# Three parts instead of two for the last output chunk of an attention and MLP kernel

## The chip, the cores and the metric

The kernel runs on one core of a Trainium2 chip. A core has TensorE (matrix products into PSUM, the accumulator memory), VectorE, ScalarE and GpSimd for element work, and SyncE (SP), whose queue issues the DMA transfers here. The profile calls them PE, DVE, ACT, POOL and SP. Each engine works through its own stream of instructions in order; between engines, semaphores tell what is done. The metric is the device time of one execution in microseconds (us), the median over runs.

## The reference

Eight batches with twelve heads of 448 tokens and 64 dimensions: queries and keys are normalised, attention is computed, the heads are put side by side to 768 columns, and an MLP with the activation h - tanh(h) follows. All is float32.

```python
attn = softmax(scale * rmsnorm(q, g_q) @ rmsnorm(k, g_k).T) @ v      # (8, 12, 448, 64)
x = attn.transpose(0, 2, 1, 3).reshape(3584, 768)
h = x @ w_in                                                         # (3584, 2048)
out = (h - tanh(h)) @ w_out                                          # (3584, 768)
```

## The kernel before

The attention of a head pair of one batch is a step; the MLP of the batches before it is cut up into single matrix products and laid between the attention's work, so that TensorE is nearly always busy. The MLP is computed with hidden units or output columns on the partitions and tokens along the rows, so the output comes out turned: 128 output columns by 448 tokens for each of the six chunks (`CD`) of a batch. It has to be turned back before it is stored.

Batches 2 to 7 are taken in pairs, and their second MLP product is a fast matrix multiplication in two levels: seven outer products `p`, in the order `OUTER = (1, 2, 3, 7, 6, 5, 4)`, each of which has two output chunks by seven inner products `q` (`ORDER`) and a third chunk (`HC - 1`) by one plain product over eight row blocks (`HF`). `project_pair` does this. `matmuls` (L1140) issues the products of one bank, `add` (L1148) is an addition on VectorE, `combine_outer` (L1151) gathers the outer products into `acc` and `acc2` and leaves later work in the lists `calm` and `todo`, which `flush` (L1202) works off, an entry at a time.

The end of the program is the last outer product of the last pair (`p == 4` with `late["ending"]`, L1253). By then four chunks remain. Two of `p == 5` and two of `p == 4` have been turned by VectorE in blocks of 32 by 32 (L1167, L1168, L1172), and ScalarE copies them into rows of 128 columns (`move_rows`, L991 to L999, four copies each), so that a store has runs of 512 bytes. The two stores of `p == 4` wait in `late["rows"]`.

The last chunk, the third one of `p == 4`, goes another way. It is cut by tokens into parts. For each part, the loop of L1259 takes a bank, issues eight products (`matmuls`, L1142), adds the bank to `acc` (L1264, L1149), turns the part straight into rows by four transposes of VectorE, one for each block of 32 columns, and issues its store on SP (`turn_rows`, L1001 to L1008; `store_rows`, L985). The first entry of `late["rows"]` is stored ahead of the loop (L1258), the second one after the first part (L1266). So SP's queue at the end is: the two copied chunks of `p == 5`, the first copied chunk of `p == 4`, the first part, the second copied chunk of `p == 4`, the remaining part.

The three banks of the products are taken in turn (`mm_bank`, L215). Each entry below runs in program order; nothing reorders it (`tc.manual_schedule()`). DMA transfers take eight semaphores in turn, and SP waits for the last use of one before it takes it again. After the program's last store, every engine branches over the code of a second, more general path to the closing code (L1843, L1875).

Of the kernel before, what the change touches and what calls it, by code (L numbers as in the profile page):

```python
# [147 lines left out]
def bounded_path(tc, ctx, q, k, v, moe_w_in, moe_w_out, out, g_col, ident, ones, half_ones, neg_half, early):  # L148
# [18 lines left out]
    B, H, S, D = q.shape  # L167
    DFF, DM = moe_w_out.shape
    P = 128
# [45 lines left out]
    def mm_bank():  # L215
        return bank_of("mm")
# [203 lines left out]
    def ring_load(to):  # L420

        for n in range(len(ring_tiles), min(to, len(ring_steps))):
            b, layer, j, p = ring_steps[n]
            t = ring_tiles[ring_steps[n]] = ring_slot()
            if layer == 0:
                assert kept[1] > j
                nc.sync.dma_start(out=t[:, : 2 * HALF], in_=w_in_dram[j, p])
            elif layer == 2 and p == 0:
                nc.sync.dma_start(out=t, in_=w_out_dram[:, BLOCKS[j], HC - 1].rearrange("p f d -> p (f d)"))
            elif layer == 2:  # L430
                n = min(2 * HB, 7 * HB - 2 * (p - 1) * HB)
                at = 2 * (p - 1) * HB
                nc.sync.dma_start(out=t[:, :n], in_=inner_dram[j][:, at : at + n])
            else:
                nc.sync.dma_start(out=t, in_=w_out_dram[:, BLOCKS[p], j].rearrange("p f d -> p (f d)"))
# [383 lines left out]
    def part(name):  # L819
        if name == "th" and "blocks" in late:  # L820
            late["turn"] = (late.get("turn", 0) + 1) % 3
            if late["turn"] == 0:
                return late["blocks"].tile([P, 2, HS], F32, name="th_more")
        return tp.tile([P, 2, HS], F32, name=name)
# [153 lines left out]
    def row_room():  # L978
        if late["places"] % 4 == 0:
            late["place"] = pp.tile([P, 2, 2, S], F32, name="p", bufs=2)  # L980
        g = late["places"] % 4
        late["places"] += 1
        return late["place"][g * BL : (g + 1) * BL].rearrange("t a b s -> t (a b s)").rearrange("t (j d) -> t j d", d=P)
# [17 lines left out]
    def turn_rows(b, n, y, room, cols):  # L1001

        for i in range(P // BL):
            nc.vector.transpose(
                out=room[:, cols.start // BL : cols.stop // BL, i * BL : (i + 1) * BL],
                in_=y[i * BL : (i + 1) * BL, cols].rearrange("d (j t) -> d j t", t=BL),
            )
        store_rows(b, n, room, cols)  # L1008

    def step_out(by=1):  # L1010
        for entry in late["out"]:
            entry[0] -= by
        while late["out"] and late["out"][0][0] <= 0:
            late["out"].pop(0)[1]()
# [60 lines left out]
    def rows(p, f, n, cols):  # L1075
        which, half = HOME[p]
        return late["pair_g"][which][:, half * HF + f : half * HF + f + n, cols]
# [35 lines left out]
    def project_pair(b, ks):  # L1113
# [15 lines left out]
        def at(k, q):  # L1129

            p = OUTER[k]
            if q in outer_plan.get(p, {}):
                outer_sum(*outer_plan[p][q])
            if k == SOON and q == 1:
                inner_sum(p, 2)
                inner_sum(p, 3)
            if q in inner_at and k + 1 in ks:
                inner_sum(OUTER[k + 1], inner_at[q])

        def matmuls(bank, n, w, moving, first):  # L1140
            for i, mv in enumerate(moving):
                nc.tensor.matmul(  # L1142
                    bank[:, :n], lhsT=w(i), rhs=mv, start=(first and i == 0), stop=(i == len(moving) - 1),
                    skip_group_check=not first,
                )
                yield 4 * n / ENGINE_NS

        def add(out, x, y, op=ALU.add):  # L1148
            nc.vector.tensor_tensor(out=out, in0=x, in1=y, op=op)  # L1149
# [52 lines left out]
        def flush():  # L1202
            now, late["todo"] = late["todo"], []
            for fn in now:
                fn()
            calm_step(p == 4 and q in (3, 7, 4))

        for k in ks:
            p = OUTER[k]
            late["ending"] = b + 2 == B and k >= len(OUTER) - 2  # L1210
            step = ring_steps.index((b, 2, p, 1))
            if p in (1, 3):
                y1, y2 = ((acc if p == 1 else acc2)[:, m] for m in range(2))
            else:
                y1, y2 = (part(n).rearrange("p f s -> p (f s)") for n in ("s2", "s5"))
            s1 = part("s1").rearrange("p f s -> p (f s)")
            banks = {}
            for i, q in enumerate(ORDER):
                ring_load(step + 5 + i // 2)
                step_out()  # L1220
                w = ring_tiles[b, 2, p, 1 + i // 2][:, i % 2 * HB : (i % 2 + 1) * HB].rearrange("p (f d) -> p f d", d=P)
                first = q not in (2, 3, 7)
                bank = banks[q] = mm_bank() if first else banks[{2: 1, 3: 5, 7: 6}[q]]
                if q in (1, 2, 3):
                    moving = [rows(p, KB * (q > 1) + c, 1, high if q == 3 else low)[:, 0] for c in range(KB)]
                else:
                    u = us.pop((p, inner_plan[q])) if q != 5 and q != 6 else us[p, inner_plan[q]]
                    moving = [u[:, c] for c in range(KB)]
                yield from matmuls(bank, HS, lambda c: w[:, c], moving, first)
                flush()  # L1230
                v = bank[:, :HS]
                if q == 1:
                    nc.scalar.copy(out=s1[:, low], in_=v)
                elif q == 5:
                    add(y2[:, low], v, s1[:, low])
                elif q == 6:
                    add(y1[:, high], v, s1[:, low])
                elif q == 2:
                    nc.scalar.copy(out=y1[:, low], in_=v)
                elif q == 7:  # L1240
                    add(y2[:, high], v, y2[:, low])
                    add(s1[:, low], v, s1[:, low])
                elif q == 3:
                    add(y1[:, high], v, y1[:, high])
                    late["todo"].append(lambda p=p, y=y1: combine_outer(p, 0, y))
                elif q == 4:
                    add(y2[:, low], v, s1[:, low])
                    late["todo"].append(lambda p=p, y=y2: combine_outer(p, 1, y))
                at(k, q)
            ring_load(step + 9)  # L1250
            step_out()
            w = ring_tiles[b, 2, p, 0].rearrange("p (f d) -> p f d", d=P)
            if p == 4 and late["ending"]:  # L1253
                while calm or late["todo"]:
                    flush()
                step_out(9)
                y, room = acc[:, HC - 1], row_room()
                late["rows"].pop(0)()  # L1258
                for cols in (slice(0, S - P), slice(S - P, S)):  # L1259
                    bank = mm_bank()  # L1260
                    moving = [rows(p, f, 1, cols)[:, 0] for f in range(HF)]
                    n = cols.stop - cols.start
                    yield from matmuls(bank, n, lambda i: w[:, i], moving, True)
                    add(y[:, cols], bank[:, :n], y[:, cols])  # L1264
                    turn_rows(b, CD - 1, y, room, cols)
                    if late["rows"]:  # L1266
                        late["rows"].pop(0)()
                continue
            bank = mm_bank()
            yield from matmuls(bank, S, lambda i: w[:, i], [rows(p, f, 1, slice(0, S))[:, 0] for f in range(HF)], True)  # L1270
            flush()
            late["todo"].append(lambda p=p, v=bank[:, :S]: combine_outer(p, HC - 1, v))
# [607 lines left out]
```

## Time and profile before

| | |
|---|---|
| median of 3 runs | 1345.73 us (1344.27 to 1347.03) |
| the profiled execution | 1345.78 us |
| its span, first to last instruction | 1344.0 us |
| granted TensorE clock, mean | 0.996 |
| last matmul starts | 1334.17 us |
| VectorE's last instruction ends | 1336.95 us |
| DMA over the span | 187 GB/s |

All times inside the execution are counted from the first instruction. The span is what the profile covers; 1.8 us of the measured time lie around it. A busy share is an average over the whole span, while the change touches its last 16 us alone, so the stages that matter are read from the timeline and from the chain of waits (which follows the end back to what released it). "Idle before" is the time an engine stood still before an instruction, with the instruction it waited for. A DMA issue is listed with the time that SP spent on it; the data move later. The fields of a matrix product are its moving operand's columns: an f32 product of 128 rows comes as two instructions.

### The profile page before, as it was taken

How to read it: one execution, taken by the hardware profiler on the slowest of the kernel's cores; microseconds unless marked ns; L12 is line 12 of the kernel's file. 1: busy time of each engine (PE TensorE's matmuls, PEld its weight loads, DVE VectorE, ACT ScalarE, POOL GpSimd, SP SyncE). 2: the span in 40 equal slices, each digit the busy share in tenths (PEclk: the TensorE clock that was granted, in tenths of full speed). 3: DMA queues.
4: the chain of work that ended last, by engine and by line, in shares of the span. 5: the costliest groups of instructions: out<-in, count | busy, mean ns of one | idle time of the engine just before them, and what ended most of it. 6: DMA issues, size and time to landing. Idle time of an engine off the chain costs nothing.

```text
span 1344.0 us, 29262 instructions
## 1 busy us (share of the span) xinstructions
PE 1311.7 (98%) x11352; PEld 1032.5 (77%) x11352; DVE 965.0 (72%) x1405; ACT 567.8 (42%) x1328; POOL 791.5 (59%) x591
## 2 busy tenths in 40 slices
PE   7988999999999999999999999999999999999997
PEld 3467854488898888688877788779887888799985
DVE  4999978867766677678888576768887667633454
ACT  7855654244333454446322345454512254311102
POOL 4766766348756256826698245944699254812761
PEclk9999999999999999999999999999999999999999
DMA  7879888889989766476655867476645775365544
GB/s 174 193 196 261 267 260 229 246 273 283 326 280 285 190 165 172 118 184 158 175 146 135 202 162 177 124 169 168 179 138 140 150 201 164 111 165 178 171 143 88
DMA packets 364744, 253.54 MB, mean 189 GB/s; under 512 B 273012, under 2 KB 303284, under 8 KB 364596
## 3 DMA queue, kind: packets, MB, share of 16 engines
q1 hardware_dynamic: 364592, 251.57, 67.6%
q8 instruction: 92, 1.51, 0.5%
q14 instruction: 56, 0.46, 0.1%
q10 hardware_dynamic: 4, 0.00, 0.0%
HBM read 205.23 MB, written 46.27 MB: 187 GB/s over the span
## 4 chain that ended last, share of the span: by engine, by line
PE 85%; DVE 5%; POOL 4%; DMA 2%; issue 1%; SPq 1%; ACT 1%; DVEq 0%; ACTq 0%; POOLq 0%
PE mm L857 39%; PE mm L1142 20%; PE sc L569 9%; PE sc L635 6%; PE mm L1339 5%; POOL u L1099 2%; PE sc L623 1%; POOL rr_mine L523 1%; PE mm L677 1%; PE sc L677 1%; PE mm L700 1%; DVE rows L613 1%; DMA qk_nat<-in_q_dram 1%; DMA w_f<-w_in 0%; DVE rows L606 0%
## 5 line engine op out<-in xcount | busy, mean ns | idle before, releaser
L857 PE MATMUL mm<-xT,w_f 128*128 128x224 f32 x1296 | 263.7, 353 | 1.1 <-DMA w_f<-w_in 1.0
L857 PEld LDWEIGHTS mm<-xT,w_f 128*128 128x128 f32 x1296 | 244.7, 190 | 6.1 <-issue 4.0
L569 PE MATMUL sc<-qT,kT 64*32 64x448 f32 (+1 forms) x3072 | 214.7, 500 | 2.8 <-ACT p_last L575 2.2
L857 PE MATMUL mm<-tt,w_f 128*128 128x224 f32 x1044 | 212.7, 355 | 0.0
L857 PEld LDWEIGHTS mm<-tt,w_f 128*128 128x128 f32 x1044 | 195.8, 190 | 15.6 <-issue 15.4
L523 POOL TENSOR_TENSOR rr_mine<-rr_mine,neg_half 128x28 f32<-128x28 f32 x33 | 161.4, 4890 | 2.8
L762 DVE TENSOR_TENSOR xT<-xT,sc 128x448 f32<-128x448 f32 x34 | 21.0, 618 | 165.9 <-PE sc L569 116.6
L1142 PE MATMUL mm<-u,w_f 128*128 128x224 f32 x672 | 137.2, 354 | 1.0 <-POOL u L1099 0.5
L905 POOL TENSOR_TENSOR gT<-s,th 128x448 f32<-128x448 f32 x44 | 57.5, 1308 | 131.8 <-ACT th L904 128.4
L1142 PE MATMUL mm<-gT,w_f 128*128 128x224 f32 (+3 forms) x496 | 132.0, 420 | 1.3 <-DVE acc L1149 0.9
L1142 PEld LDWEIGHTS mm<-u,w_f 128*128 128x128 f32 x672 | 126.1, 190 | 8.0 <-POOL u L1099 3.6
L569 PEld LDWEIGHTS sc<-qT,kT 64*32 64x32 f32 x3072 | 72.1, 106 | 67.3 <-issue 49.6
L1142 PEld LDWEIGHTS mm<-gT,w_f 128*128 128x128 f32 x496 | 92.5, 190 | 35.9 <-issue 32.0
L635 PE MATMUL sc<-p,v_nat 64*32 64x448 f32 x1184 | 116.9, 536 | 0.0
L1142 PE MATMUL mm<-g,w_f 128*128 128x224 f32 (+1 forms) x360 | 98.9, 428 | 0.0
L575 ACT ACTIVATE p<-sc 128x448 f32<-128x448 f32 x132 | 71.7, 543 | 50.4 <-PE sc L569 36.0
L905 POOL TENSOR_TENSOR g<-s,th 128x448 f32<-128x448 f32 x24 | 30.3, 1262 | 104.1 <-ACT th L904 104.1
L1142 PEld LDWEIGHTS mm<-g,w_f 128*128 128x128 f32 x360 | 67.9, 190 | 26.5 <-issue 26.0
L729 ACT COPY sum_g<-sum 32x14 f32<-32x14 f32 x280 | 56.3, 201 | 71.0 <-DVE sum L721 65.3
L1339 PE MATMUL mm<-gT,w_out 128*128 128x448 f32 x192 | 74.0, 542 | 0.0
L145 POOL TENSOR_TENSOR rr<-rr,neg_half 112x8 f32<-112x8 f32 (+1 forms) x30 | 49.4, 1677 | 35.7 <-DVE rr L144 35.2
L1099 POOL TENSOR_TENSOR u<-gT 128x448 f32<-128x448 f32 x48 | 63.4, 1341 | 11.1 <-PE mm L1142 11.1
(206 smaller groups left out, 2461.8 us busy)
## 6 DMA issues: line engine op xcount, KB each, us to landing
w_f<-w_in SPq DMA_DIRECT2D x196, 384.0 KB, 3.4
w_f<-w_inner SPq DMA_DIRECT2D x63, 512.0 KB, 3.6
w_f<-w_out SPq DMA_DIRECT2D x42, 512.0 KB, 4.0
w_raw<-in_moe_w_out_dram SPq DMA_DIRECT2D x16, 768.0 KB, 5.4
w_in<-w_out SPq DMA_DIRECT2D x21, 384.0 KB, 5.2
qk_nat<-in_q_dram SPq DMA_DIRECT2D x132, 56.0 KB, 2.7
qk_nat<-in_k_dram SPq DMA_DIRECT2D x132, 56.0 KB, 2.3
g<-w_out SPq DMA_DIRECT2D x14, 512.0 KB, 5.4
```

Source lines behind the costliest of these rows:

```text
L145: nc.gpsimd.tensor_tensor(out=r, in0=r, in1=neg_half[:rows], op=ALU.pow)
L523: nc.gpsimd.tensor_tensor(out=mine, in0=mine, in1=neg_half[:, :1].to_broadcast([P, 2 * NJ]), op=ALU.pow)
L569: nc.tensor.matmul(tiles[h][i * BL : (i + 1) * BL, :n], lhsT=kT[r, c * P + at : c * P + at + BL], rhs=qT[r, first : first + n], start=True ...
L575: nc.scalar.activation(p[:, h, c if c < 2 else 0, :], tiles[h][:, :n], AF.Exp, scale=1.0 if rr is None else rr[:, 0, 2 * c + h : 2 * c + h ...
L635: nc.tensor.matmul(av[g][i * BL : (i + 1) * BL, :S], lhsT=v_nat[keys, h, c, m * BL : (m + 1) * BL], rhs=p[keys, h], start=first, stop=True ...
L677: nc.tensor.matmul(av[n][r : r + BL, :HS], lhsT=v_nat[:, h, c, m * BL : (m + 1) * BL], rhs=p[c][:, h, n * HS : (n + 1) * HS], start=False, ...
L729: nc.scalar.copy(out=acc[h * BL : (h + 1) * BL, g], in_=part[g * BL : (g + 1) * BL, h * NJ : (h + 1) * NJ])
L857: nc.tensor.matmul(bank[:, f * HS : (f + 1) * HS], lhsT=w[:, c * width + f, :], rhs=moving[p](c), start=(first and f == 0 and c == 0), sto ...
L905: eng.tensor_tensor(out=g[:, rows, cols], in0=h, in1=th, op=ALU.subtract)
L1099: nc.gpsimd.tensor_tensor(out=u[:, half], in0=a[:, half], in1=z[:, half], op=ALU.subtract)
L1142: nc.tensor.matmul(bank[:, :n], lhsT=w(i), rhs=mv, start=(first and i == 0), stop=(i == len(moving) - 1), skip_group_check=not first,)
L1339: nc.tensor.matmul(bank[:, :S], lhsT=w_out_row(f, n // HC)[:, n % HC * P : (n % HC + 1) * P], rhs=g[:, f, :], start=(f == 0), stop=(f == C ...
```

## The change

The loop over the parts of the last chunk runs over three slices of tokens, 192, 128 and 128, where it ran over two, 320 and 128. With `S = 448` and `P = 128`:

```diff
@@ -1256,7 +1256,7 @@
                 step_out(9)
                 y, room = acc[:, HC - 1], row_room()
                 late["rows"].pop(0)()
-                for cols in (slice(0, S - P), slice(S - P, S)):
+                for cols in (slice(0, S - 2 * P), slice(S - 2 * P, S - P), slice(S - P, S)):
                     bank = mm_bank()
                     moving = [rows(p, f, 1, cols)[:, 0] for f in range(HF)]
                     n = cols.stop - cols.start
```

The body of the loop is the same. Each part has its own bank, eight products, an addition, four transposes and a store; the second copied chunk of `p == 4` is still stored after the first part, and so ahead of the second one and the third.

## The prediction

> **What bounds the kernel now.** I read the page first, then the chain of waits of the last 44 us, then the timeline of the last 19 us by shape, and last SP's issues one by one. The page says TensorE, and the chain of waits (start, length, what) says where that stops:
>
> ```profile
> PE 1311.7 (98%) x11352; PEld 1032.5 (77%) x11352; DVE 965.0 (72%) x1405; ACT 567.8 (42%) x1328; POOL 791.5 (59%) x591
> ```
>
> ```profile
> by line: PE mm L1142 75.1%; DVE p L1004 6.8%; DVE acc L1149 1.8%; issue 1.1%
> ...
> 1299.65 33.02 PE mm L1142 x148
> ...
> 1332.70 0.50 DVE acc L1149
> ...
> 1333.23 0.50 DVE p L1004
> ...
> 1335.34 0.30 DVE acc L1149
> ...
> 1336.65 0.30 DVE p L1004
> ```
>
> TensorE carries the chain up to 1332.68. From there it is VectorE: add of 320 columns, four transposes, add of 128, four transposes, to 1336.95. The change lies wholly in this tail, so nothing before 1328.19 can move. The timeline by shape (start, busy, engine, line, what, count):
>
> ```profile
> 1328.19 6.25 PE L1142 MATMUL mm<-gT,w_f 128*128 128x320 f32 x32
> 1328.70 7.01 ACT L995 COPY p<-s 32x448 f32<-32x448 f32 x12
> ...
> 1330.54 0.65 DVE L1172 STREAM_TRANSPOSE s<-acc 128x448 f32<-128x448 f32 x1
> 1332.70 0.49 DVE L1149 TENSOR_TENSOR acc<-mm,acc 128x320 f32<-128x320 f32 x1 [1.52 <-PE mm L1142]
> 1333.23 2.08 DVE L1004 STREAM_TRANSPOSE p<-acc 32x320 f32<-32x320 f32 x4
> 1335.34 0.29 DVE L1149 TENSOR_TENSOR acc<-mm,acc 128x128 f32<-128x128 f32 x1
> 1335.66 1.29 DVE L1004 STREAM_TRANSPOSE p<-acc 32x128 f32<-32x128 f32 x4
> ```
>
> The first row holds both parts (16 instructions of each shape). VectorE idles 1.52 us before the first add: this is what a smaller first part can use. ACT is busy until 1335.71 with the copies of two other chunks, whose stores share SP's queue with ours. SP's single issues:
>
> ```profile
> 1333.39 0.32 SPq L986 DMA_DIRECT2D out_dram<-p  x1
> ...
> 1335.33 0.32 SPq L986 DMA_DIRECT2D out_dram<-p  x1
> ...
> 1335.74 0.41 SPq L986 DMA_DIRECT2D out_dram<-p  x1
> ...
> 1336.98 0.90 SPq L986 DMA_DIRECT2D out_dram<-p  x1
> ...
> 1319.92 1.38 SPq L971 DMA_DIRECT2D out_dram<-s  x1
> ```
>
> In order: the store of the copied chunk 3 (R1), of our 320 tokens, of the copied chunk 4 (R2), of our last 128 tokens, and an older store for comparison. An undisturbed issue takes 0.32 us. The last one took 0.90 us: SP was held 0.58 us. After it SP has only its branch (1337.93) and the closing waits; the first of these ran at 1340.49, the second at 1342.69, and the span ends at 1344.0. So the end follows SP's last issue by 6.1 us (1344.0 - 1337.88), and that issue is the number to predict.
>
> The hold has a visible cause. The DMA view of 1336 to 1337.5 lists instruction packets among the stores:
>
> ```profile
> q8 instruction: 1, 0.02, 4.7%
> q14 instruction: 2, 0.02, 2.6%
> ```
>
> The q8 packet (16 KB, one DMA engine) ran from 1336.36 to 1337.49. On 15 engines our 320-token store had landed by 1337.84, on the sixteenth at 1338.75, and SP's last issue went through at 1337.88, 0.39 us after the packet. The older store shows the same: q8 packet from 1319.57 to 1320.87, the third store of a row through at 1321.30, 0.42 us after it. A third store in flight waits until the slowest engine has worked off enough of the first two.
>
> [...]start to start 0.269 us at 320 columns[...] and 0.1117 at 128[...]. [...]transposes of 320 and 128 columns take 0.500 and 0.300 us, that is 1.04 ns per column on 0.167 us. [...]SP's 2.56 us between branch and first closing wait holds an 8 KB instruction packet at 1338.85. No run shows whether the page position of that code matters.
>
> **The change part by part.**
>
> TensorE: 32 instructions become 48. [...]First part: 16 x 0.1625 = 2.60, so its data are ready at 1328.19 + 2.60 + 0.19 (the lag seen before: 1332.496 to 1332.68) = 1330.98. Second: + 16 x 0.1117 = 1332.77. Third: 1334.55, 0.1 us later than now. The third bank is that of product 4, read last by the add at 1328.40: no wait.
>
> VectorE: one add and four transposes more. Add of 192: 0.292 + 64 x (0.493 - 0.292)/192 = 0.359. Transpose of 192: 0.367. With the gaps of now (0.147 in the group of five): first group 0.359 + 1.467 + 0.147 = 1.97 us. A group of 128 lasts 1335.34 to 1336.95, 1.61, plus 0.03 to the next. The first add can't start before the transpose of line 1172 ends (1331.19), which is later than its data. So: 1331.19, second add 1333.16 (data 1332.77), third 1334.81 (data 1334.55), end 1336.42, against 1336.95: 0.53 us earlier. The 1.51 us won at the start pay for 0.98 us of added instructions. All of TensorE's added time is hidden under VectorE by 0.26 us; without that cover it would cost at most 0.1.
>
> SP: the first part's store is ready at 1333.14 but stands behind R1, which waits for ACT until 1333.39; it costs nothing, as it is through long before R2. R2 waits for ACT until 1335.71 as now. The second part's store (ready about 1334.78) stands behind R2 and goes at 1336.15 (R2's 1335.74 + 0.32 + the 0.09 between two issues). The third waits for VectorE until 1336.45 and for the second's issue until 1336.47 + 0.09 = 1336.56. Unheld it is through at 1336.88: 1.0 us before the 1337.88 of now. Nothing is queued behind it but the branch. POOL has no work here.
>
> The hold is the unknown. The q8 packet comes 0.6 us after TensorE's last marker and so moves by 0.1, to about 1336.46 to 1337.59. R2's packets (28 per engine) arrive from 1336.55, after it has begun, so one engine keeps nearly all of R2 until 1337.59, then R2, the second and the third store. Lower end: 28 + 8 packets per engine fit where 20 + 28 did not, no hold, -1.0 us. Upper end: SP is held until R2 is through on that engine, as it was for our 320-token store now: 0.4 to 0.6 us after 1337.59, by the two holds above and the larger packets, 1338.0 to 1338.2, +0.3 at most. In between, it is released when a handful of R2's packets are off: 0.1 us after the packet ends, 1337.69. I take this, -0.2 us, since the sum in flight is smaller than in both holds but the blocked engine is the same.
>
> Landing stays covered: the blocked engine has 44 packets, at the 23.5 ns between the packets of the last engine at work now, 1.03 us after 1337.59, and about 0.6 us to land (1339.14 to 1339.74 now): 1339.2, before the first closing wait.
>
> **Sum.** 1345.78 (profiled execution: span 1344.0 and 1.8 around it) - 0.2 = 1345.6; that execution is 0.05 above the median, so 1345.73 - 0.2 = 1345.5.
>
> **The rivals.**
> - Full gain: no hold, VectorE's 0.53 us and the old hold are both won, -1.0: 1344.7. For: small stores. Against: the same engine is blocked by the instruction packet.
> - Slower: the last store is held until R2 is through on the blocked engine. Place: SP's third issue behind R2; price +0.3: 1346.0. It decides as soon as R2 arrives after the instruction packet and the hold asks for the first of two stores to be done. For: both holds seen end about there. Against: only 8 packets stand between.
> - The closing code: SP's stream grows by a store and a wait, so the code after the branch shifts. If the 2.2 us between the two closing waits (1340.49, 1342.69) is a page boundary, it can go: -2.2 or, with the full gain, -3.2: 1343.5 or 1342.5. Against: all engines fetch twice after their branch, so the second fetch may be fixed. The reverse, a new stall of this size, is as thinly supported.
> - The change does what it says: three stores will be seen.
>
> **How the numbers follow.** Forecast 0.45, slower 0.22, full gain 0.22, closing code 0.11 (mostly the faster side). Runs of the kernel before scatter from 1344.27 to 1347.03, so 0.2% (2.7 us) is about what a measurement can tell from no change. Only the closing code, or scatter, passes it: faster 0.10, same 0.84, slower 0.06. The range takes in full gain and slower rival with 0.8 us of scatter each: 1343.9 to 1346.9.
>
> **What would show it.** First add of 192 at 1331.2 with almost no idle time before it; VectorE's last transpose ending at 1336.4; matmuls of 192 columns 0.1625 us apart; SP's last issue starting near 1336.6 and through between 1336.9 and 1338.2, with its length as the verdict on the hold; 6.1 us from there to the end. I am wrong if VectorE ends later than 1336.7, if that 6.1 us changes, or if the end ceases to follow SP's last issue.

## The result and the profile after

| | before | three parts |
|---|---|---|
| median, 22 runs each | 1344.95 us (1343.19 to 1348.60) | 1342.59 us (1340.91 to 1348.29) |
| ratio to before | | 0.9985, interval 0.9979 to 0.9991 |
| span of the profiled execution | 1344.0 us | 1340.7 us |
| first matmul of the last chunk | 1328.19 us | 1326.57 us |
| from there to the end of the span | 15.8 us | 14.2 us |

In this measurement the change makes the kernel faster by 1.2 to 2.8 us, under 0.2% in the middle. The 1342.59 us lie below the range that was forecast, 1343.9 to 1346.9 us. The last row is the one to work with. Up to the last chunk both kernels run the same instructions, and that stretch scatters from execution to execution: in the ten profiles of this study it ends between 1325.97 and 1332.00 us, with two parts as well as with three. So from here on, times are counted from the first matmul of the last chunk, called M, and the tail is the stretch from M to the end of the span.

The page has the same busy time of TensorE; its 16 new instructions are lost in it, so nothing is to be read there:

```profile
PE 1311.5 (98%) x11368; PEld 1033.4 (77%) x11368; DVE 969.5 (72%) x1410; ACT 568.1 (42%) x1328; POOL 795.0 (59%) x591
```

The chain of waits after the change (start, length, what) has no idle time of VectorE ahead of the last chunk any more:

```profile
1319.92 6.83 PE mm L1142 x36
...
1328.91 0.65 DVE s L1172
1329.56 0.25 DVE acc L1149
...
1331.39 0.30 DVE acc L1149
...
1333.02 0.30 DVE acc L1149
...
1334.34 0.30 DVE p L1004
```

Before, TensorE carried the chain to 4.5 us after M. Now VectorE has it from 0.2 us on, and its last transpose ends at M + 8.08 (1334.65 less 1326.57) where it ended at M + 8.76. The timeline by shape shows the pieces:

```profile
1326.57 6.33 PE L1142 MATMUL mm<-gT,w_f 128*128 128x192 f32 x48
...
1329.48 0.32 DVE L1149 TENSOR_TENSOR acc<-mm,acc 128x192 f32<-128x192 f32 x1
1329.83 1.53 DVE L1004 STREAM_TRANSPOSE p<-acc 32x192 f32<-32x192 f32 x4
1331.39 0.29 DVE L1149 TENSOR_TENSOR acc<-mm,acc 128x128 f32<-128x128 f32 x1
1331.72 1.27 DVE L1004 STREAM_TRANSPOSE p<-acc 32x128 f32<-32x128 f32 x4
1333.02 0.29 DVE L1149 TENSOR_TENSOR acc<-mm,acc 128x128 f32<-128x128 f32 x1
1333.35 1.29 DVE L1004 STREAM_TRANSPOSE p<-acc 32x128 f32<-32x128 f32 x4
```

So VectorE gains 0.7 us. SP's issues show that none of it arrives at the end of SP's queue (copied chunk 3, first part, copied chunk 4, second part, third part):

```profile
1331.77 0.32 SPq L986 DMA_DIRECT2D out_dram<-p  x1
...
1332.17 1.16 SPq L986 DMA_DIRECT2D out_dram<-p  x1
...
1334.11 0.32 SPq L986 DMA_DIRECT2D out_dram<-p  x1
...
1334.52 1.07 SPq L986 DMA_DIRECT2D out_dram<-p  x1
...
1335.68 0.68 SPq L986 DMA_DIRECT2D out_dram<-p  x1
```

The first part's store is held (1.16 us for an issue of 0.32), without harm, since it is through before the second copied chunk is ready. The second part's store is held too (1.07 us), and so is the third (0.68). The 16 KB instruction packet of queue 8, which the prediction took for the cause of the hold, runs beside the last two as it did before, from M + 8.36 to 9.54:

```profile
q8 instruction: 1, 0.02, 1.1%
```

So the last issue is through at 1336.36, M + 9.79. Before it was 1337.88, M + 9.69. At SP's last store, then, the changed kernel is 0.1 us late. Its gain comes after that, in code which the change doesn't touch. The view of the closing code's line (engine, instruction, count, duration in ns, first and last start) says where. Before, up to 1342.5 us and then all of them:

```profile
L1875 SPq EVENT_SEMAPHORE  x1: 28/28/28, 1340.5 to 1340.5; - x1
...
L1875 SPq EVENT_SEMAPHORE  x10: 17/28/28, 1340.5 to 1343.9; - x10
```

After:

```profile
L1875 SPq EVENT_SEMAPHORE  x10: 17/28/28, 1339.4 to 1340.7; - x10
```

SP's ten closing waits take 3.4 us before and 1.3 us after. Before, the first one runs at 1340.49 and the second at 1342.69, though the last store had landed by 1339.74; after, they follow each other by 0.08 us. That is 2.1 us won. The wait between SP's branch and its first closing wait is 0.4 us longer (2.98 for 2.56, the ends of the range in which the profiles below have it), and the last issue 0.1 us later: together -1.6 us, the whole difference of the tails.

### The profile page after: what moved, and what is told of

Read it like the earlier page. It is cut to its first block, busy times and chain, and to the rows that moved or that the text cites. A ratio compares the mean times of both kernels' runs of the same rounds, so it can differ in the third digit from the quotient of the medians.

```text
span 1340.7 us, 29301 instructions
## 1 busy us (share of the span) xinstructions
PE 1311.5 (98%) x11368; PEld 1033.4 (77%) x11368; DVE 969.5 (72%) x1410; ACT 568.1 (42%) x1328; POOL 795.0 (59%) x591
## 3 DMA queue, kind: packets, MB, share of 16 engines
q8 instruction: 92, 1.51, 0.5%
## 4 chain that ended last, share of the span: by engine, by line
PE 83%; DVE 7%; POOL 4%; DMA 2%; SPq 2%; issue 2%; ACT 1%; DVEq 0%; ACTq 0%; POOLq 0%
PE mm L857 38%; PE mm L1142 21%; PE sc L569 9%; PE sc L635 6%; PE mm L1339 5%; POOL u L1099 3%; PE sc L623 1%; POOL rr_mine L523 1%; PE sc L677 1%; DVE w_out L357 1%; PE mm L677 1%; SPq L497 1%; DVE rs L705 1%; DMA w_f<-w_inner 1%; DVE w_out L82 0%
## 5 line engine op out<-in xcount | busy, mean ns | idle before, releaser
L857 PEld LDWEIGHTS mm<-tt,w_f 128*128 128x128 f32 x1044 | 195.8, 190 | 15.9 <-issue 15.4
```

Source lines behind the costliest of these rows:

```text
L857: nc.tensor.matmul(bank[:, f * HS : (f + 1) * HS], lhsT=w[:, c * width + f, :], rhs=moving[p](c), start=(first and f == 0 and c == 0), sto ...
```

## The experiments

Two readings were open. **Page**: the profile of the kernel before counts 92 instruction packets of 16 KB on queue 8 (1.51 MB) and 56 of 8 KB on queue 14 (0.46 MB); what one packet brings is called a page here. One of 8 KB runs within the pause behind the first closing wait, from 1341.04 to 1341.60 us. By this reading the pause is the fetch of the next page, since a page of SP's stream ended just there; the change adds two instructions to SP's stream (a store and a wait), which moves the closing code onto the next page. **Split**: the three parts themselves bring the gain. SP's stream holds, in this order, the path that runs, the path that never runs (396 instructions) and the closing code. Instructions put into the path that never runs shift the closing code (its distance in instructions is counted in slots here) and leave what runs as it is.

Each ratio compares with runs of the kernel before that were made together with the experiment. Their median was 1345.69 us for the two slots, the first attempt and the two kernels of "No fetch behind the branch", and 1344.60 us for the other timed ones, so medians from different experiments are not to be compared. Every tail and every row of the table below comes from one profiled execution.

**Two slots for the kernel before.**

```diff
     with cmp.Else():
         with ExitStack() as arm:
+            for _ in range(2):
+                nc.sync.drain()
             make_g_col()
```

> The kernel before with two idle instructions put into SP's code of the other, never executed path, so that only the place of the closing code in SP's stream moves by two slots[...]. Page theory (the second closing wait sits on the far side of a page boundary in the kernel before): the 2.17 us between the first and the second closing wait fall to under 0.1 us, and the time falls by 1.5 to 2.3 us, ratio 0.9983 to 0.9989. Rival (the split of the last chunk itself made the kernel faster): no change, the 2.17 us stay, ratio 1.0000 within 0.0006.

Measured: ratio 0.9986 (0.9979 to 0.9993), the same as for the change, with nothing of the last chunk altered. The closing waits:

```profile
L1877 SPq EVENT_SEMAPHORE  x10: 17/28/28, 1344.2 to 1345.5; - x10
```

They take 1.3 us, the tail 13.6 us. M is at 1332.00 in this execution, which is why its clock times lie above those of the kernel before. Page holds: two slots, in SP's stream alone, bring the gain without the split (a tail of 13.6 us for 15.8).

**The changed kernel put back, first attempt.**

```diff
+            for _ in range(126):
+                nc.sync.nop(nofuse=True)
             make_g_col()
```

> The changed kernel (three parts) with 126 idle instructions in SP's code of the never executed path, which puts the closing code back on the slot that it had in the kernel before. Page theory: a pause of about 2.2 us is back between the first and the second closing wait, and the time is that of the kernel before within 0.0006 (ratio 0.9994 to 1.0006), 1.5 to 2.3 us over the changed kernel. Rival (the split is what helps): ratio 0.9985 as for the changed kernel, no pause.

It tested nothing: idle instructions of this kind are dropped when the program is put together, so SP's code of the path that never runs still had 396 instructions. It is the changed kernel once more, with a tail of 14.1 us and no pause, and a ratio of 0.9997 (0.9989 to 1.0006) where the first measurement had given 0.9985. The tails of the kernel before and the changed one give 0.9988 (1.6 of 1345 us), inside the first interval and just below the second. That shows how far a ratio can be trusted here.

**The changed kernel put back, with instructions that are kept.**

```diff
+            for _ in range(130):
+                nc.sync.drain()
             make_g_col()
```

With the 130 kept instructions, four of SP's own waits in that path fall away, so the closing code lies 126 slots later than in the changed kernel, 128 later than in the kernel before. That 128 slots lead to an equal place was not shown before this run.

> The changed kernel with idle instructions in SP's code of the never executed path, of a kind that is kept in the program[...]. Page theory: a pause of about 2.2 us is back between the first and the second closing wait, and the stretch from the first matmul of the last chunk to the end is 14.2 (changed kernel) + 2.2 - 0.1 to 0.5 (the fetch after the branch ends somewhat earlier) = 15.9 to 16.4 us, so no shorter than the 15.8 of the kernel before; time ratio 0.9995 to 1.0010. Rival (the split does it): no pause, 14.2 us.

Measured: ratio 1.0006 (0.9998 to 1.0014), tail 15.9 us. The closing waits up to 1342.3 us, then all of them:

```profile
L1877 SPq EVENT_SEMAPHORE  x1: 27/27/27, 1340.4 to 1340.4; - x1
...
L1877 SPq EVENT_SEMAPHORE  x10: 17/28/28, 1340.4 to 1343.7; - x10
```

One wait, a pause of 2.02 us, and the rest: the pause is back and the gain of the three parts is gone.

**The pause moved.** The loop of the first experiment with `range(127)`: 124 slots for the kernel before.

> The kernel before with its closing code moved by 124 slots, so that five closing instructions lie ahead of the page boundary instead of one. Page theory: the pause moves, from between the first and the second closing wait to between the fifth and the sixth, and is shorter by the 0.25 us that four more waits take: about 1.9 us. Rival (the pause belongs to the branch or to the first wait, not to a boundary): it stays behind the first wait or is gone.

This kernel was profiled once and not timed. The closing waits up to 1340.5 us and from there on:

```profile
L1877 SPq EVENT_SEMAPHORE  x5: 28/28/28, 1338.7 to 1339.0; - x5
...
L1877 SPq EVENT_SEMAPHORE  x5: 17/28/28, 1340.8 to 1341.8; - x5
```

Five, a pause of 1.73 us (1.9 expected), five. The pause sits on a place in the stream and not on a wait. A shift of 128 puts it back (2.02 us, behind the first wait), and one of 124 brings four more instructions ahead of it (1.73 us, behind the fifth), which fits places that repeat every 128 instructions. These shifts would fit a divisor such as 64 as well; which of them it is was not shown.

The page of each profile counts these 8 KB packets. The kernel before, the changed one, and the changed one of the next experiment have:

```profile
q14 instruction: 56, 0.46, 0.1%
...
q14 instruction: 55, 0.45, 0.1%
...
q14 instruction: 53, 0.43, 0.1%
```

All three profiles with the pause have 56, and all four that keep the jump but have no pause have 55: with the pause, one packet more is counted.

**No fetch behind the branch.** The three DMA lines of the path that never runs are issued by ScalarE, so that one SP instruction is left between the branch and the closing code. Both kernels:

```diff
-            nc.sync.dma_start(
+            nc.scalar.dma_start(
...
-                nc.sync.dma_start(out=out[r0 : r0 + P, d], in_=o_sb)
+                nc.scalar.dma_start(out=out[r0 : r0 + P, d], in_=o_sb)
...
-                    nc.sync.dma_start(out=out[r0 : r0 + REST, d], in_=o_sb[i * REST : (i + 1) * REST])
+                    nc.scalar.dma_start(out=out[r0 : r0 + REST, d], in_=o_sb[i * REST : (i + 1) * REST])
```

> The changed kernel with the transfers of the never executed path issued by ScalarE instead of SP, so that only one SP instruction lies between SP's last branch and the closing code. If SP's 2.98 us between its branch and its first closing wait are the fetch of a page that the branch jumps to, the first closing wait now runs as soon as the last store has landed, about 1.3 to 1.7 us earlier against the first matmul of the last chunk than in the changed kernel, and the time is 1341.0 to 1341.6 where the kernel before has 1344.95 (ratio 0.997). If the 2.98 us are the landing of the store or a fixed cost of the branch, no change against the changed kernel, ratio 0.9985.

> The kernel before (two parts) with the same move of the never executed path's transfers to ScalarE. Page theory: both pauses go, 3.5 to 4 us less than before after SP's last issue, only the landing of the last store is left, ratio 0.9972 to 0.9980. Against the three parts with the same move it tells what the split is worth when no fetch lies behind it: theory 0 to 0.3 us either way, rival that the split helps by 1 us or more: this kernel is 1 us or more over the three parts.

Measured: three parts 1343.54 us, ratio 0.9983 (0.9976 to 0.9990), tail 13.1 us; two parts 1342.75 us, ratio 0.9982 (0.9973 to 0.9991), tail 13.0 us. The three profiles without the jump have 53 packets of 8 KB, two fewer than the changed kernel, and between SP's branch and its first closing wait one packet is left of two. With three parts the first closing wait comes 1.55 us earlier against M, as expected. But both ratios lie above those that were expected. The landing takes the fetch's place, and more of it was left than was thought: with three parts the first and second closing waits run at M + 11.27 and 11.80, each 0.01 to 0.02 us after the last DMA engine of the second and third store has reported; with two parts the first runs at M + 11.61, 0.01 us after the last store. So the end gains 1.06 us with three parts, and with two parts the stretch behind SP's last issue shrinks by 2.2 us instead of 3.5 to 4. And with no fetch behind it, the split is worth nothing: the tail is 0.15 us longer with three parts.

**Two stores for three parts.** The second and third part are multiplied, added and turned apart, but stored as one; two slots of shift as in the first experiment, to keep the closing code on the changed kernel's page.

```diff
-    def turn_rows(b, n, y, room, cols):
+    def turn_rows(b, n, y, room, cols, stored=True):
...
-        store_rows(b, n, room, cols)
+        if stored:
+            store_rows(b, n, room, slice(cols.start - (P if cols.stop == S else 0), cols.stop))
...
-                    turn_rows(b, CD - 1, y, room, cols)
+                    turn_rows(b, CD - 1, y, room, cols, cols.stop - cols.start != P or cols.stop == S)
```

> Three parts as in the changed kernel, but the second and the third are stored together, as 256 tokens, after the third (closing code on the slot of the changed kernel). Theory that SP's last issue is held by the two stores ahead of it: only one store is now in flight ahead of it, it starts at 8.26 us after the first matmul of the last chunk (VectorE's end is 8.08) instead of 9.11 and takes 0.32 us instead of 0.68, SP's branch comes at 8.6 instead of 9.84, and with the same wait for the fetch (2.6 to 3.0) the stretch to the end is 12.8 to 13.1 us instead of 14.2. Rival (the hold belongs to the blocked DMA engine, however many stores are in flight): the issue is held until about 9.8 again, 14.1 us.

Measured: 1342.67 us, ratio 0.9983 (0.9975 to 0.9992), tail 13.2 us. SP's last issue:

```profile
1334.62 0.92 SPq L986 DMA_DIRECT2D out_dram<-p  x1
```

It starts at M + 8.11, right behind VectorE, but is held all the same, 0.60 us, and is through at M + 9.02, where the three stores are through at 9.79. The tail lies between the 12.8 to 13.1 us that were expected and the rival's 14.1. The later half of the expectation missed: one whole store ahead is enough for a hold. The changed kernel's first part showed this already: of the stores ahead of it, only the copied chunk 3, issued 0.09 us earlier, was still under way.

**Both together.** The two stores and ScalarE's issues.

> The same two stores for three parts, and the transfers of the never executed path issued by ScalarE, so that SP fetches nothing after its branch. Theory: only the landing of the last store is left; 28 + 16 packets on the DMA engine that an instruction packet blocks until about 9.6 us, landed at 11.0 to 11.6, and 1.35 us to the end: 12.4 to 12.9 us from the first matmul of the last chunk, against 12.95 for two parts with the same move, the fastest of all; ratio 0.9972 to 0.9982. Rival (the landing comes later, since the last store is twice as large): 13.1 us or more, no better than two parts.

Measured: 1342.65 us, ratio 0.9985 (0.9978 to 0.9991), tail 12.4 us, the shortest of all.

```profile
1334.08 0.35 SPq L986 DMA_DIRECT2D out_dram<-p  x1
...
L1876 SPq EVENT_SEMAPHORE  x10: 17/28/28, 1337.0 to 1338.3; - x10
```

The last issue (M + 8.11) is hardly held, and the first closing wait runs at M + 11.08, 0.02 us after the landing. It beats both kernels by the tail, 3.4 us against before and 1.8 against the changed one; by the ratio it is faster than before and can't be told from the changed kernel. The tail is in the range that was expected, 12.4 to 12.9 us, while the ratio lies above the expected 0.9972 to 0.9982. The tails alone would give 0.9975 (3.4 of 1345 us), just below the measured interval, so this ratio is no measure of the last microsecond either.

Where SP's closing code stands alike, the three parts with two stores have a shorter tail than two parts: 13.20 for 13.58 us with two slots, 12.42 for 12.96 with the other queue. In these single executions the finer split brings 0.4 to 0.5 of VectorE's 0.68 us, once it adds no store.

All tails in one table, one execution each. The ends and "through", the end of SP's last issue, are in us after M; the wait behind the branch and the pause are lengths in us. A cell marked "landing" is a wait that ended with a store's landing:

| kernel | VectorE ends | last issue through | branch to first closing wait | pause | end |
|---|---|---|---|---|---|
| before | 8.76 | 9.69 | 2.56 | 2.20, behind the first | 15.79 |
| before, 2 slots | 8.76 | 9.46 | 2.72 | none | 13.58 |
| before, 124 slots | 8.76 | 9.45 | 2.78 | 1.73, behind the fifth | 15.37 |
| before, other queue | 8.76 | 9.10 | 2.46 (landing) | none | 12.96 |
| three parts | 8.08 | 9.79 | 2.98 | none | 14.17 |
| three parts, again | 8.08 | 9.90 | 2.80 | none | 14.10 |
| three parts, put back | 8.07 | 9.83 | 2.75 | 2.02, behind the first | 15.93 |
| three parts, other queue | 8.08 | 10.01 | 1.21 (landing) | 0.53 (landing) | 13.11 |
| two stores | 8.08 | 9.02 | 2.78 | none | 13.20 |
| two stores, other queue | 8.08 | 8.45 | 2.57 (landing) | none | 12.42 |

## Why the prediction was wrong

**TensorE and VectorE: right.** The sum took 0.1625 us for a matmul of 192 columns, which the profile before does not show; in the changed kernel these matmuls follow each other by 162.5 ns. A straight line through the spacings before, 0.269 us at 320 columns and 0.1117 at 128, gives 164. All three parts span 6.33 us, 0.08 more than two (0.1 forecast), hidden under VectorE. VectorE ends at M + 8.08 for a forecast of 8.23 (1336.42 less 1328.19); it saves 0.68 us instead of 0.53, because the first add overlaps the end of the transpose ahead of it (M + 2.91 for 3.00) and its group takes 1.91 us for 1.97.

**SP's queue: the place right, the share of the hold too small.** The second part's store goes at M + 7.95, as forecast (1336.15 is M + 7.96), behind the copied chunk. The third was to be through between 8.7 and 10.0 and taken at 9.5. All four profiles with three stores have it between 9.79 and 10.01, near the end that the slower rival named. That rival was right about the split: with the place of the closing code equal, three parts have the longer tail by 0.59 us (14.17 for 13.58), 0.14 (15.93 for 15.79) and 0.15 (13.11 for 12.96). What the forecast missed here is that the second store is held as well as the third. Its rule, that a third store in flight waits for the first two, does not hold either: the first part's store was held behind one, and the last store of two parts with the other queue was not held behind two (0.32 us).

**The 6.1 us from SP's last issue to the end: this is the step that failed.** The sum carried them over unchanged. The prediction named a change of it as one of the things that would prove it wrong. They are 4.4 us in the changed kernel (14.17 less 9.79), and shifting the closing code by two slots takes the same term from 6.1 to 4.1 in the kernel before. The rival about the closing code named this mechanism and its 2.2 us, and had a chance of 0.11. The reason given against it, that every engine fetches twice after its branch, was no argument. In all seven profiles with the jump, with the pause and without it, an 8 KB packet starts 0.54 to 0.56 us after SP's first closing wait. A pause came with it only in the three where, by the shifts, SP's code goes on across the boundary at once: there the next wait runs 1.0 to 1.1 us after that packet's end. An 8 KB packet follows VectorE's first closing instruction too (before, the instruction is at M + 10.87 and the packet at 11.46), but then VectorE waits for SP until 15.20. In the kernel before, the two packets that are put down to SP (1338.85 and 1341.04) both come behind its one branch (1337.93), and the second is not covered: SP stands for 2.2 us. A shift of 128 slots brings that pause back (2.02 us).

The prediction knew that SP's stream grows by two instructions. Where a page of SP's stream begins was not worked out ahead of the result, and it stays open whether the profile before would have told it.

## What to carry to other kernels

An edit of a few instructions can be worth more by where it moves the code behind it than by what it does (here two slots alone take the tail from 15.79 to 13.58 us): before a gain in a tail is credited to a change, shift the code by the same number of instructions in a path that never runs. In a tail, look beyond the last transfer: here SP's branch, the two packets behind it and the closing waits took 6.1 us, more than the 4.3 us of VectorE's work that was being tuned (1332.70 to 1336.95). And here a finer split brought nothing while it added a store to a queue that was held (tails longer by 0.14 to 0.59 us), though VectorE was done 0.68 us earlier.

## What was not expected of the hardware

The pause of 1.7 to 2.2 us appears in the three kernels in which the page boundary of SP's stream lies, by the shifts, behind the first or the fifth closing instruction, and is absent in the seven other profiles. With a jump over the other path's transfers, SP's first closing wait came 2.56 to 2.98 us after its branch, later than the landing each time. With a jump over one instruction it came 0.01 to 0.02 us after the landing, at the least 1.21 us after the branch.

What holds SP's late issues is not settled. The prediction put it down to the 16 KB instruction packet that blocks one DMA engine. But in the kernel before with two slots of shift that packet began at M + 9.29, after the last issue had started (8.79) and close to when it went through (9.46), and in the two parts with the other queue it began at 8.86 and the issue of 8.79 wasn't held at all (0.32 us). How long the hold lasts varies from 0 to 0.9 us in places that are otherwise alike. A kernel without this packet was not tried.
